# Two scatter views, later weight loads, and a middle layer among the last gates, in an attention and mixture-of-experts kernel

## The chip, the cores and the metric

The kernel runs on one core of one Trainium2 chip. A core has a matrix engine (TensorE, PE in the profile; PEld is its weight load), a vector engine (VectorE, DVE), a scalar engine (ScalarE, ACT), a general engine (GpSimd, POOL) and a queue engine (SyncE, SP), which here mainly starts DMA transfers. A letter q behind an engine's name (POOLq, SPq) stands for its sequencer. The metric is the device time of one execution in microseconds (us). A profiled execution gives the trace from which the tables below come.

## The reference

The reference is an attention block followed by a mixture of experts. The attention has 8 batches of 8 heads, 576 positions of 64 numbers; half of the heads see the last 32 positions, the other half every 32nd. Its output x (4608 rows of 512 numbers) goes to the experts. Every row takes one of 8 experts, and each expert is two layers with a ReLU between them:

```python
logits = np.einsum('bsd,de->bse', x, w_gate)
local_gate = 1.0 / (1.0 + np.exp(-np.einsum('bsd,de->bse', x, w_local).squeeze(-1)))
for b in range(B):
    prev_e = -1
    for s in range(S):
        fresh_e = int(np.argmax(logits[b, s]))
        if s == 0 or local_gate[b, s] < 0.5:
            e = fresh_e
        else:
            e = prev_e if prev_e >= 0 else fresh_e
        prev_e = e
        ...                                     # p = softmax(logits[b, s])
        h = np.maximum(x[b, s] @ w1[e], 0.0)    # 512 -> 1024
        out[b, s] = p[e] * (h @ w2[e])          # 1024 -> 512
```

So a row keeps the expert of the row before it unless its local gate is under one half. All is in 32-bit floats.

## The kernel before

The kernel computes the attention, two heads at a time ("pairs" of heads, 32 in all), stores x to a buffer xd in HBM, and works out the choice of each row: `gates` multiplies x by the gate weights, `choices` turns the result into codes and probabilities, and `route` sorts the rows by expert into tiles of 128. An expert tile then gathers its rows from xd by an indirect DMA (`gather`), turns them with the PE's transpose (`turn_x`), runs the first layer (`hidden`), the second (`output`), scales by the probability and scatters the rows to the output with an indirect DMA (`scatter`). Six tiles of the first three batches come first (units 0 to 5); they fill the time in which the last choices are routed. Then come pairs of tiles that share an expert (computed with seven products instead of eight), two mixed tiles between them, up to four single tiles, and at last the "late" pairs, as many as there are, each in an `If`.

The output is one tensor, and every scatter writes somewhere in it:

```python
    def scatter(self, y, rd, i):
        self.nc.gpsimd.indirect_dma_start(out=self.out, in_=y, in_offset=None, bounds_check=N - 1, oob_is_err=False,
                                          out_offset=bass.IndirectOffsetOnAxis(ap=rd.si[:, i:i + 1], axis=0))
```

The framework orders two writes of one tensor, so a scatter waits until the one before it has landed.

The end of the attention, where `n` counts pairs of heads and runs three steps past the last; `psX` is a pool of two PSUM banks that transposes, gates and choices use in turn:

```python
        done = pairs[n - 3][0].b if n >= 3 and pairs[n - 3][0].pair == PAIRS - 1 else None
        if done is not None:
            gates(done)
        yield n, st["pe"].ins
        if 0 <= n - 1 < len(pairs):
            values(pairs[n - 1][0])
        if done is not None:
            choices(done)
        if 0 <= n - 1 < len(pairs):
            u = pairs[n - 1][1]
            values(u)
            if u.i2 == 1:
                store_x(u.b, u.grp)
        if 0 <= n - 2 < len(pairs):
            u = pairs[n - 2][0]
            turn_x(u.b, u.pair)
```

`turn_x(0)` of the first expert tile is called one step before the last gates (`n == PAIRS * (B - BE) - 1` in the caller). After the attention all eight PSUM banks become one ring, `pse`; the first two are those of psX:

```python
    def later(self, ctx):
        self.banks = Banks(ctx.enter_context(self.tc.tile_pool(name="pse", bufs=1, space=PSUM)))
        self.banks.ring.used = 2
        # ... a third set of weights (w1x, w2x) and buffers of the pairs

    def hidden(self, j):
        nc, u = self.nc, self.U[j]
        w1, xT, hT = self.sets[u["set"]][0], u["xT"], u["hT"]
        for g in range(FK // self.HB):                      # two halves
            ps = self.bank()
            for i in range(self.HB):                        # four blocks of 128 in each
                c = slice((g * self.HB + i) * P, (g * self.HB + i + 1) * P)
                for kk in range(DK):
                    ins = nc.tensor.matmul(ps[:, i * P:(i + 1) * P], lhsT=w1[:, kk, c],
                                           rhs=xT[:, kk * P:(kk + 1) * P], start=(kk == 0), stop=(kk == DK - 1))
            nc.scalar.activation(hT[:, g * self.HB:(g + 1) * self.HB], ps.rearrange("p (i m) -> p i m", i=self.HB),
                                 Act.Relu)
        return ins.ins

    def output(self, j):                                     # plain tiles; mixed ones left out here
            for kk in range(FK):
                ins = nc.tensor.matmul(ps, lhsT=hT[:, kk], rhs=w2[:, kk, :], start=(kk == 0), stop=(kk == FK - 1))
        nc.scalar.activation(y, ps, Act.Copy, scale=u["pt"][:, 0:1])
        self.scatter(y, u["rd"], u["cols"][0])
        return ins.ins
```

How a unit runs and when it starts the weights of later ones (`self.last` is the first late pair; `weights(j)` gives four loads of 1 MB, two of w1 and two of w2; an `If` is opened around each `run(j)` of a late pair):

```python
    def unit(self, j, loads, nxt, step=lambda ins: None):
        # ...
        # first layer; then the first half of loads; step; turn_x of nxt; second layer; the other half; step

    def run(self, j, step=lambda ins: None):
        for k in self.gathers.get(j, []):
            self.gather(k)
        if j == self.last:
            for piece in self.weights(j + 1):
                piece()
        loads = self.weights(j + 2) if j + 2 < (self.last if j < self.last else len(self.U)) else []
        # ...
        self.unit(j, loads, self.turns.get(j, []), step)

    def early(self, second, check):
        def step(ins):
            with self.tc.issue_after(ins):
                next(second, None)
        for j in range(NE - 1):
            self.run(j, step)
        assert next(second, None) is None
        check()
```

`check` is the bounds check on the sums of the attention. Four VectorE operations (`ok` twice, `low`, `one`), one matmul and one more VectorE operation make one number, `bad`; if it isn't zero, the whole work is done again in a careful way. With these inputs it is zero.

```python
    nc.vector.tensor_scalar(ok, flat, SUM_LO, None, Alu.is_ge)
    nc.vector.scalar_tensor_tensor(ok, flat, SUM_HI, ok, Alu.is_le, Alu.mult)
    nc.vector.tensor_reduce(low, ok, axis=AX.X, op=Alu.min)
    nc.vector.memset(one, 1.0)
    nc.tensor.matmul(ps[0:1, 0:1], lhsT=low, rhs=one, start=True, stop=True)
    nc.vector.tensor_scalar(bad, ps[0:1, 0:1], -1.0, float(P), Alu.mult, Alu.add)
```

`issue_after(ins)` tells the scheduler to place what stands in the block behind the instruction named. The scheduler decides the order within each engine's queue otherwise.

Of the kernel before, what the change touches and what calls it, by code (L numbers as in the profile page):

```python
# [18 lines left out]
P = 128  # L19
# [99 lines left out]
@with_exitstack  # L119
def attention_then_scomoe(ctx: ExitStack, tc: tile.TileContext, q, k, vl, vs, wg, w1, w2, out):  # L120


    nc = tc.nc
    once = ctx.enter_context(tc.tile_pool(name="once", bufs=1))
    dram = ctx.enter_context(tc.tile_pool(name="dram", bufs=1, space=DRAM))
    xd = dram.tile([N, DX], F32, name="xd")
    c = Consts(tc, once)
    sums = once.tile([P, B * PAIRS * 2, 2, 3], F32, name="sums")
    nc.gpsimd.memset(sums, 1.0)
    bad = once.tile([1, 1], I32, name="bad")  # L130

    passes(tc, False, q, k, vl, vs, wg, w1, w2, out, xd, c, sums, bad)
    again = nc.values_load(bad[0:1, 0:1], min_val=0, max_val=P,
                           skip_runtime_bounds_check_because="a count of partitions")
    with tc.If(again > 0):
        passes(tc, True, q, k, vl, vs, wg, w1, w2, out, xd, c, sums, bad)
# [56 lines left out]
def passes(tc, careful, q, k, vl, vs, wg, w1, w2, out, xd, c, sums, bad):  # L193
    with ExitStack() as ctx:
# [7 lines left out]
        ex = Experts(ctx, tc, xd, w1, w2, out, c, r1, r2)  # L202
        with ExitStack() as part:
            psX = part.enter_context(tc.tile_pool(name="psX", bufs=2, space=PSUM))
            rp = part.enter_context(tc.tile_pool(name="rp", bufs=1))
            first = route(tc, rp, psX, BE, c, codes, r1, early)
            pieces = ex.weights(0) + ex.weights(1)
            for n, ins in attention(part, tc, careful, psX, q, k, vl, vs, wg, xd, c, codes, sums):
                n -= PAIRS * BE + 3

                if n == 0 or n >= 3:
                    with tc.issue_after(ins):
                        next(first, None)
                if n == PAIRS * (B - BE) - 1:
                    ex.banks = psX
                    ex.turn_x(0)
                if n in PIECES:
                    pieces.pop(0)()
                if 10 <= n < 10 + AHEAD:
                    ex.gather(n - 10)  # L220
        with ExitStack() as part:
            ex.later(ctx)
            rp = part.enter_context(tc.tile_pool(name="rp2", bufs=1))
            ex.early(route(tc, rp, ex.banks, B, c, codes, r2, early),
                     lambda: None if careful else bounds(tc, rp, ex.banks, sums, bad))
# [20 lines left out]
def attention(ctx, tc, careful, psX, q, k, vl, vs, wg, xd, cc, codes, sums):  # L246
# [8 lines left out]
    psS = ctx.enter_context(tc.tile_pool(name="psS", bufs=2, space=PSUM))  # L255
# [130 lines left out]
    def values(u):  # L386
# [5 lines left out]
        for h, order in ((0, reversed(range(m))), (1, range(m))):  # L392
            for i in order:
                o = (h * m + i) * V1 + (pad if h else 0)
                c = 0 if h else VW - w
                nc.tensor.matmul(ps[0:w, o:o + w], lhsT=u.e[0:kb, h, i * w:(i + 1) * w],  # L396
                                 rhs=vt[0:kb, u.i2, u.t0 + i, c:c + w], start=True, stop=True)
# [23 lines left out]
    def turn_x(b, pair):  # L421
# [7 lines left out]
        for ts in ((0, 1, 2), (3, 4, 5)) if grp == 0 else ((0, 1, 2), (3, 4)):  # L429
            w = LQ if grp == 0 else SBLK[ts[0]][1] * SP  # L430
            ps = psX.tile([P, 512], F32, name="xps")
            for i, t in enumerate(ts):
                nc.tensor.transpose(ps[:, i * w:(i + 1) * w], src[0:w, t, i2 * P:(i2 + 1) * P], ident[0:w, 0:w])  # L433
# [7 lines left out]
    def gates(b):  # L441
# [3 lines left out]
        for a in range(2):  # L445
            s = slice(a * (S // 2), (a + 1) * (S // 2))
            pg = psX.tile([P, 512], F32, name="xps")
            for kk in range(DK):
                nc.tensor.matmul(pg[kk * GC:(kk + 1) * GC, 0:S // 2], lhsT=wgs[:, kk, :], rhs=xT[:, kk, s],  # L449
                                 start=True, stop=True)  # L450
            nc.scalar.copy(out=gl[:, s], in_=pg[:, 0:S // 2])
        st["gl", b] = gl

    def choices(b):
        gl = st["gl", b]
        ps = psX.tile([P, 512], F32, name="xps")
        for t in range(LT):
            nc.tensor.matmul(ps[0:LQ, t * (E + 1):(t + 1) * (E + 1)], lhsT=gl[:, t * LQ:(t + 1) * LQ],  # L458
                             rhs=sel, start=True, stop=True)
# [36 lines left out]
    for n in range(len(pairs) + 3):  # L496
# [8 lines left out]
        done = pairs[n - 3][0].b if n >= 3 and pairs[n - 3][0].pair == PAIRS - 1 else None  # L505
        if done is not None:
            gates(done)
        yield n, st["pe"].ins
        if 0 <= n - 1 < len(pairs):
            values(pairs[n - 1][0])  # L510
        if done is not None:
            choices(done)
# [5 lines left out]
        if 0 <= n - 2 < len(pairs):  # L518
            u = pairs[n - 2][0]
            turn_x(u.b, u.pair)  # L520
# [223 lines left out]
class Experts:  # L744
# [14 lines left out]
    def __init__(self, ctx, tc, xd, w1, w2, out, c, r1, r2):  # L759
        self.tc, self.nc = tc, tc.nc  # L760
        self.xd, self.w1, self.w2, self.out, self.c = xd, w1, w2, out, c
# [36 lines left out]
        for j, u in enumerate(self.U):  # L798
# [3 lines left out]
            self.turns.setdefault(ahead - 1, []).append(j)  # L802
# [4 lines left out]
    def later(self, ctx):  # L807

        self.banks = Banks(ctx.enter_context(self.tc.tile_pool(name="pse", bufs=1, space=PSUM)))
        self.banks.ring.used = 2  # L810
# [194 lines left out]
    def hidden(self, j):  # L1005
        nc, u = self.nc, self.U[j]
        w1, xT, hT = self.sets[u["set"]][0], u["xT"], u["hT"]
        for g in range(FK // self.HB):
            ps = self.bank()
            for i in range(self.HB):  # L1010
                c = slice((g * self.HB + i) * P, (g * self.HB + i + 1) * P)
                for kk in range(DK):
                    ins = nc.tensor.matmul(ps[:, i * P:(i + 1) * P], lhsT=w1[:, kk, c],  # L1013
                                           rhs=xT[:, kk * P:(kk + 1) * P], start=(kk == 0), stop=(kk == DK - 1))
            nc.scalar.activation(hT[:, g * self.HB:(g + 1) * self.HB], ps.rearrange("p (i m) -> p i m", i=self.HB),
                                 Act.Relu)
        return ins.ins
# [18 lines left out]
    def scatter(self, y, rd, i):  # L1036
        self.nc.gpsimd.indirect_dma_start(out=self.out, in_=y, in_offset=None, bounds_check=N - 1, oob_is_err=False,  # L1037
                                          out_offset=bass.IndirectOffsetOnAxis(ap=rd.si[:, i:i + 1], axis=0))

    def unit(self, j, loads, nxt, step=lambda ins: None):  # L1040
# [7 lines left out]
        else:  # L1048
            self.end = (self.hidden_mixed if "halves" in u else self.hidden)(j)
# [13 lines left out]
    def run(self, j, step=lambda ins: None):  # L1063
# [3 lines left out]
        if j == self.last:  # L1067
            for piece in self.weights(j + 1):
                piece()
        loads = self.weights(j + 2) if j + 2 < (self.last if j < self.last else len(self.U)) else []  # L1070
# [4 lines left out]
    def early(self, second, check):  # L1075
# [9 lines left out]
        check()  # L1085
# [77 lines left out]
```

## Time and profile before

| | |
|---|---|
| device time, median of three | 706.21 us (704.58 to 706.42) |
| profiled span, first to last instruction | 704.3 us |
| mean granted TensorE clock | 0.983 |
| attention | up to about 163.7 us of the span |
| six early tiles | 163.7 to 258.6 |
| pairs and two mixed tiles | 258.6 to 571.7 |
| four single tiles | 571.7 to 629.1 |
| two late pairs | 629.1 to 680.2 |
| HBM traffic | 164.00 MB read, 19.55 MB written |

The page of the profile gives busy shares of each engine, the chain of work that ended last, and groups of instructions by line. The table of stretches cuts the span where one wants and gives busy times and the DMA share for each cut; the timeline lists instructions in order of time, with the idle time before each in brackets and what ended it. An fp32 matmul is recorded as two passes, so the 32 matmuls of one first layer appear as x64. Times in the timeline are from the start of the span.

### The profile page before, as it was taken

How to read it: one execution, taken by the hardware profiler on the slowest of the kernel's cores; microseconds unless marked ns; L12 is line 12 of the kernel's file. 1: busy time of each engine (PE TensorE's matmuls, PEld its weight loads, DVE VectorE, ACT ScalarE, POOL GpSimd, SP SyncE). 2: the span in 40 equal slices, each digit the busy share in tenths (PEclk: the TensorE clock that was granted, in tenths of full speed). 3: DMA queues.
4: the chain of work that ended last, by engine and by line, in shares of the span. 5: the costliest groups of instructions: out<-in, count | busy, mean ns of one | idle time of the engine just before them, and what ended most of it. 6: DMA issues, size and time to landing. Idle time of an engine off the chain costs nothing.

```text
span 704.3 us, 13289 instructions
## 1 busy us (share of the span) xinstructions
PE 674.3 (96%) x5258; PEld 579.0 (82%) x5258; DVE 401.4 (57%) x901; ACT 193.3 (27%) x360; POOL 102.5 (15%) x101
## 2 busy tenths in 40 slices
PE   8999999999999999999999999999999999999960
PEld 8999899987677779999499995899999986779950
DVE  6777888774374157576456955277578530307640
ACT  3454534442111123312132221313313311113310
POOL 1000002000003511120223202021122011020210
PEclk9999999999999999999999999999999999999995
DMA  9988788994878996885768767675688759468350
GB/s 344 374 305 289 228 282 294 370 329 146 306 265 291 322 398 260 275 310 218 269 246 306 250 238 278 212 229 191 210 298 293 269 181 338 162 229 309 124 207 7
DMA packets 75227, 184.01 MB, mean 261 GB/s; under 512 B 9743, under 2 KB 19471, under 8 KB 75153
## 3 DMA queue, kind: packets, MB, share of 16 engines
q1 hardware_dynamic: 68464, 162.10, 65.5%
q0 software_dynamic: 6400, 20.63, 8.4%
q8 instruction: 45, 0.74, 0.4%
q10 hardware_dynamic: 288, 0.31, 0.2%
q14 instruction: 30, 0.24, 0.1%
HBM read 164.00 MB, written 19.55 MB: 261 GB/s over the span
## 4 chain that ended last, share of the span: by engine, by line
PE 65%; issue 16%; DMA 11%; DVE 4%; ACT 1%; POOL 0%; SPq 0%; POOLq 0%; DVEq 0%
PE bank L896 32%; PE vps L396 9%; DMA out_dram<-y,si 7%; PE bank L1013 6%; PE bank L1031 6%; PE sps L349 5%; PE bank L1027 2%; PE xps L433 2%; DMA w2t<-in_w_dram 2%; DMA w1t<-in_w_dram 1%; PE xps L449 1%; PE xps L458 1%; DMA vlt<-in_vl_dram 1%; DMA xd<-ex 0%; DVE e L356 0%
## 5 line engine op out<-in xcount | busy, mean ns | idle before, releaser
L1037 POOL DMA_INDIRECT out_dram<-y,si x38 | 49.9, 1312 | 291.7 <-DVE y L964 135.5
L839 POOL DMA_INDIRECT xg<-xd,gi x42 | 49.4, 1175 | 288.8 <-DMA xd<-ex 114.1
L1013 PEld LDWEIGHTS bank<-xgT,w1t 128*128 128x128 f32 x640 | 72.6, 192 | 2.4 <-issue 1.9
L1013 PE MATMUL bank<-xgT,w1t 128*128 128x128 f32 x640 | 73.6, 276 | 0.3 <-DVE lt L461 0.3
L1031 PE MATMUL bank<-w2t,hT 128*128 128x512 f32 x160 | 70.3, 592 | 0.0
L1031 PEld LDWEIGHTS bank<-w2t,hT 128*128 128x128 f32 x160 | 29.6, 190 | 33.5 <-issue 33.5
L931 DVE TENSOR_TENSOR part<-bank,part 128x512 f32<-128x512 f32 x13 | 9.0, 692 | 80.6 <-ACT part L928 80.6
L896 PE MATMUL bank<-xs,t 128*128 128x128 f32 x416 | 50.7, 275 | 0.0
L896 PE MATMUL bank<-t,hs 128*128 128x256 f32 x208 | 49.2, 379 | 0.2 <-DVE hs L870 0.2
L896 PEld LDWEIGHTS bank<-xs,t 128*128 128x128 f32 x416 | 48.5, 192 | 0.0
L896 PEld LDWEIGHTS bank<-xT,w1t 128*128 128x128 f32 x384 | 45.7, 192 | 2.6 <-issue 2.1
L896 PE MATMUL bank<-xT,w1t 128*128 128x128 f32 x384 | 47.4, 276 | 0.0
L896 PE MATMUL bank<-xs,w1t 128*128 128x128 f32 x384 | 46.8, 275 | 0.0
L921 DVE TENSOR_TENSOR h<-bank,part 128x512 f32<-128x512 f32 x39 | 27.0, 692 | 34.7 <-ACT part L933 22.9
L349 PE MATMUL sps<-qt,kt 64*128 64x96 f32 (+2 forms) x704 | 45.7, 275 | 0.7 <-issue 0.6
L896 PE MATMUL bank<-w2t,h 128*128 128x256 f32 x192 | 45.4, 379 | 0.0
L896 PE MATMUL bank<-w2t,hs 128*128 128x256 f32 x192 | 45.4, 379 | 0.0
L896 PEld LDWEIGHTS bank<-xs,w1t 128*128 128x128 f32 x384 | 44.8, 192 | 0.0
L349 PEld LDWEIGHTS sps<-qt,kt 64*128 64x128 f32 (+2 forms) x704 | 40.1, 183 | 5.3 <-issue 3.2
L896 PEld LDWEIGHTS bank<-t,hs 128*128 128x128 f32 x208 | 39.4, 190 | 5.9 <-issue 0.6
L961 ACT ACTIVATE part<-bank,pt 128x256 f32<-128x256 f32 x39 | 18.5, 475 | 92.4 <-PE bank L896 92.4
L353 ACT ACTIVATE e<-sps 128x576 f32<-128x576 f32 (+1 forms) x64 | 40.0, 651 | 12.6 <-PE sps L349 12.2
(280 smaller groups left out, 1108.9 us busy)
## 6 DMA issues: line engine op xcount, KB each, us to landing
w1t<-in_w_dram SPq DMA_DIRECT2D x52, 1024.0 KB
w2t<-in_w_dram SPq DMA_DIRECT2D x52, 1024.0 KB
kt<-in_k_dram SPq DMA_DIRECT2D x15, 608.0 KB
qt<-in_q_dram SPq DMA_DIRECT2D x15, 576.0 KB
vlt<-in_vl_dram SPq DMA_DIRECT2D x8, 780.0 KB
w1x<-in_w_dram SPq DMA_DIRECT2D x6, 1024.0 KB
w2x<-in_w_dram SPq DMA_DIRECT2D x6, 1024.0 KB
vst<-in_vs_dram SPq DMA_DIRECT2D x8, 650.0 KB
```

Of the source, the lines that this page charges most:

```text
L349: st["pe"] = nc.tensor.matmul(ps[0:kb, h, i * w:(i + 1) * w], lhsT=kt[r, u.i2, c:c + kb], rhs=qt[r, u.i2, c:c + w], start=True, stop=True)
L353: nc.scalar.activation(ev, ps[0:kb, :, 0:m * w], Act.Exp, bias=0.0, scale=1.0 / DH ** 0.5)
L396: nc.tensor.matmul(ps[0:w, o:o + w], lhsT=u.e[0:kb, h, i * w:(i + 1) * w], rhs=vt[0:kb, u.i2, u.t0 + i, c:c + w], start=True, stop=True)
L433: nc.tensor.transpose(ps[:, i * w:(i + 1) * w], src[0:w, t, i2 * P:(i2 + 1) * P], ident[0:w, 0:w])
L839: self.nc.gpsimd.indirect_dma_start(out=u["xg"][:, a] if "pair" in u else u["xg"], out_offset=None, in_=self.xd[0:u["rows"]], in_offset=ba ...
L896: self.end = fn(*args, **kw).ins
L921: nc.vector.tensor_tensor(to, ps, add, op=Alu.add)
L961: nc.scalar.activation(to, ps, Act.Copy, scale=g[r])
L1013: ins = nc.tensor.matmul(ps[:, i * P:(i + 1) * P], lhsT=w1[:, kk, c], rhs=xT[:, kk * P:(kk + 1) * P], start=(kk == 0), stop=(kk == DK - 1))
L1027: ins = nc.tensor.matmul(ps[s], lhsT=hT[:, kk, s], rhs=w[:, kk, :], start=(kk == 0), stop=(kk == FK - 1))
L1031: ins = nc.tensor.matmul(ps, lhsT=hT[:, kk], rhs=w2[:, kk, :], start=(kk == 0), stop=(kk == FK - 1))
L1037: self.nc.gpsimd.indirect_dma_start(out=self.out, in_=y, in_offset=None, bounds_check=N - 1, oob_is_err=False, out_offset=bass.IndirectOff ...
```

## The change

The change has four parts.

- The output is split into two views that the framework takes as disjoint, and the scatters write them in turn. A scatter then waits for the last but one and not for the last. (The rows of two scatters are never the same, as every row has one tile.) The careful second pass begins with a read of both views, so that it waits for the scatters of the first.
- A late pair starts the four loads of the next late pair only, at its own beginning. Before, the first late pair started those of the second and, half by half, of the third, and so on.
- The first layer of the first expert tile is cut into four pieces of two blocks and put among the last transposes, gates and choices of the attention, pinned one behind the other, with its results in the PSUM banks of the attention's scores. `turn_x(0)` comes two steps earlier, and `turn_x(1)` right after the last choices. The ring of eight banks starts at the seventh.
- The bounds check is put in an `issue_after` block behind the last instruction of the early tiles.

```diff
+    views = dram_disjoint_views(out, 2)
+    passes(tc, False, q, k, vl, vs, wg, w1, w2, views, xd, c, sums, bad)
     ...
     with tc.If(again > 0):
+        seen = once.tile([1, 2], F32, name="seen")
+        for i, v in enumerate(views):
+            nc.gpsimd.dma_start(out=seen[:, i:i + 1], in_=v[0:1, 0:1])
+        nc.gpsimd.tensor_copy(seen, seen)
     ...
     def scatter(self, y, rd, i):
-        self.nc.gpsimd.indirect_dma_start(out=self.out, in_=y, ...
+        self.views.append(self.views.pop(0))
+        self.nc.gpsimd.indirect_dma_start(out=self.views[0], in_=y, ...
```

```diff
     def run(self, j, step=lambda ins: None):
-        if j == self.last:
+        if self.last <= j < len(self.U) - 1:
             for piece in self.weights(j + 1):
                 piece()
-        loads = self.weights(j + 2) if j + 2 < (self.last if j < self.last else len(self.U)) else []
+        loads = self.weights(j + 2) if j + 2 < self.last else []
```

```diff
+            psS = part.enter_context(tc.tile_pool(name="psS", bufs=2, space=PSUM))
+            fill = ex.begin(psS)
     ...
-                if n == PAIRS * (B - BE) - 1:
+                if n == PAIRS * (B - BE) - 3:
                     ex.banks = psX
                     ex.turn_x(0)
     ...
+            ex.turn_x(1)
     ...
+    def filling():
+        with tc.issue_after(st["end"].ins):
+            st["end"] = next(fill)
+
+    def after():
+        return tc.issue_after(st["end"].ins)
     ...
+        last = done == B - 1
         if done is not None:
-            gates(done)
+            with after() if last else nullcontext():
+                gates(done)
         yield n, st["pe"].ins
         if 0 <= n - 1 < len(pairs):
             values(pairs[n - 1][0])
+        if last:
+            filling()
         if done is not None:
-            choices(done)
+            with after() if last else nullcontext():
+                choices(done)
+        if last:
+            filling()
     ...
         if 0 <= n - 2 < len(pairs):
             u = pairs[n - 2][0]
-            turn_x(u.b, u.pair)
+            if n - 1 == len(pairs):
+                filling()
+                with after():
+                    turn_x(u.b, u.pair)
+                filling()
+            else:
+                turn_x(u.b, u.pair)
     ...
-        self.banks.ring.used = 2
+        self.banks.ring.used = 6
     ...
+    def begin(self, pool):
+        for i, self.begun in enumerate(self.hidden_blocks(0, pool)):
+            if i % 2:
+                yield self.begun
     ...
         # in early():
-        check()
+        with self.tc.issue_after(self.end):
+            check()
```

`hidden_blocks` is `hidden` as a generator: it yields after each block of four matmuls and can take its PSUM from a pool that is passed in. `st["end"]` is set by the matmuls of values, transposes, gates and choices.

## The prediction

> **What bounds the kernel now.** I read the page's busy shares first, then the table of stretches, then the timeline at the two places where TensorE (PE) is not busy, then the chain of waits.
>
> ```profile
> PE 674.3 (96%) x5258; PEld 579.0 (82%) x5258; DVE 401.4 (57%) x901; ACT 193.3 (27%) x360; POOL 102.5 (15%) x101
> ```
>
> PE is the bound: 674.3 of 704.3 us. So a change that leaves PE's work as it is, as this one does, can win at most the 30.0 us in which PE is idle. The table of stretches says where they are (columns: stretch, length, then busy time of PE, PEld, DVE, ACT, POOL, granted clock, DMA share, GB/s).
>
> ```profile
> 17.60:152.00 134.40, 133.28 (x1619) 120.76 (x1619) 101.56 (x357) 64.88 (x132) 4.09 (x4) 0.99 0.89 307
> 152.00:164.00 12.00, 10.56 (x103) 8.49 (x101) 6.39 (x24) 4.97 (x10) 0.08 (x1) 1.00 0.73 245
> 164.00:258.60 94.60, 94.60 (x604) 69.91 (x603) 44.12 (x119) 11.82 (x20) 21.84 (x17) 1.00 0.82 291
> ...
> 572.00:629.00 57.00, 57.00 (x331) 41.76 (x330) 7.59 (x13) 7.26 (x12) 5.96 (x6) 1.00 0.65 230
> ```
>
> PE never stops between 164.0 and 680.2 but for some 0.9 us in all at the mixed tiles. The change touches two of the idle places: the hand-over from attention to experts (152 to 164) and the end (680.2 to 704.3, 24.1 us without one matmul). First the hand-over, in the timeline (start, us, engine, line; in brackets the idle time before and who ended it):
>
> ```profile
> 158.83 0.87 PE L433 MATMUL xps<-ident,xs 108*128 108x108 f32 x5 [0.58 <-ACT xT L439]
> 160.12 1.59 PE L449 MATMUL xps<-xT,wgs 128*32 128x288 f32 x16 [0.42 <-ACT xT L439]
> 163.69 7.41 PE L1013 MATMUL bank<-xgT,w1t 128*128 128x128 f32 x64 [0.30 <-DVE lt L461]
> 167.78 0.36 DVE L235 TENSOR_SCALAR ok<-sums 128x384 f32<-128x384 f32 x1 [3.51 <-DMA xd<-xs]
> 169.13 0.51 DVE L238 TENSOR_REDUCE low<-ok 128x1 f32<-128x384 f32 x1
> 169.56 0.20 DVE L479 TENSOR_TENSOR codes<-code,fr 96x48 f32<-96x48 f32 x1
> ```
>
> See that the bounds check (ok, low) already lies inside the chain of the last choices here: VectorE stood 3.51 us until the stores of xs had landed. It did no harm, because PE had 7.41 us of the first middle layer to do meanwhile and wanted codes only at 171.03. Then the end:
>
> ```profile
> 675.01 5.55 SPq L830 DMA_DIRECT2D w2t<-in_w_dram  x2
> ...
> 680.24 0.47 ACT L961 ACTIVATE y<-bank,pt 128x256 f32<-128x256 f32 x1 [2.97 <-PE bank L896]
> 682.64 1.01 POOL L1037 DMA_INDIRECT out_dram<-y,si  x1 [3.55 <-DMA out_dram<-y,si]
> ```
>
> The last y is there at 680.71, but its scatter starts at 682.64: it waited for the scatter before it. The list of DMA issues for the last 24 us gives its landing, and the list of the If's control instructions what GpSimd does then:
>
> ```profile
> out_dram<-y,si POOLq DMA_INDIRECT x1, 6.6
> ```
>
> ```profile
> L226 POOLq EVENT_SEMAPHORE  x4: 17/43/6563, 682.6 to 689.4; - x4
> L226 POOLq INC_SWDGE_SEM  x1: 1780/1780/1780, 689.4 to 689.4; - x1
> ```
>
> 6.6 us to land, at 689.24; GpSimd stands in a wait of 6.56 us for it and goes on at 689.4. From there 15.06 us of control work lead to 704.3. Beside the scatter the DMA engines still load w2t: the second of the two issues at 675.01 came at 680.2, and 683 to 685 shows 418 GB/s. It is for the third of the late pairs, which does not exist with these inputs: only two late pairs run (PE reads w1x, then w1t, and then ends).
>
> [...] the scatter at 652.61 lands after 2.77 us in the chain of waits. [...] what stands behind a waiting instruction waits too. The 3.51 us above show it.
>
> **The change part by part.** PE's work is the same instructions, so each part is worth only the idle time it removes.
>
> *Two views.* The last scatter no longer waits for the one before. The one before started 0.28 us after its y (y ended 677.31 + 0.48 = 677.79, start 678.07). So the last starts at 680.71 + 0.28 = 680.99 and not at 682.64: 1.65 us on the path. Elsewhere the waits between scatters sum to 13.6 us (17.2 in all less this 3.6), but GpSimd stood there off the path, since PE had no idle time: 0.
>
> *Weights one pair ahead.* In the first late pair nothing moves: the built order has the same eight loads after one another, only the If test of the second pair now stands between them. The four loads for a third pair (w1t from 658.29, w2t from 675.01) leave the second pair's block and stand behind a test that fails: 4 MB are not loaded. With the DMA engines empty the last scatter should land in 2.77 instead of 6.6 us: 3.8 us on the path.
>
> *A side effect.* The build also puts six of the eight output matmuls of the third single tile behind the whole block of the fourth. Same work, same PE time; the fourth tile's xgT is needed at 608.18 + 2 x 0.86 = 609.9 and is there (its transposes end at 608.2, the copy takes 0.69). I count 0[...].
>
> *First middle layer among the gates.* What it fills: from 155.50 to 163.69 are 8.19 us, and the work in it, from the chain of waits, is 2.25 (values) + 0.44 (transposes of xg, at their undisturbed length) + 0.50 + 0.50 (transposes of xs) + 1.11 (gates, undisturbed as at 29.27) + 0.95 (choices) = 5.75. So 2.44 us can be filled, and the 64 passes of the middle layer (7.14 us, 111.6 ns each) are more than enough. What it costs: with these passes spent early, PE comes to the output layer at 155.50 + 5.75 + 7.14 + 0.44 (transposes of the second tile) = 168.85, and that stands on PSUM bank 0, where the second tile's transposes have just been written. It has to wait until VectorE has copied them away. In the built VectorE order this copy stands behind ok, gmx, fr, ok, ex, eq, low, eq, gsm, code, gsm, one, code, gsm: the pin on the bounds check has not moved it behind the choices; it now stands right after lt, ahead of gmx. The first ok again waits for the stores of xs. Those come some 0.4 us later than before (the copy of the first xgT and two small operations now go ahead of the last xs on VectorE), so ok starts at about 168.1. From ok to the copy, in steps of start to start as the timeline before has them (0.28 and 0.47 for the two ok, 0.43 for low, 0.05 to 0.13 for the rest): 2.3 us, so the copy runs from 170.4 to 171.1. PE stands from 168.85 to 171.15, 2.3 us. Then one output matmul (0.86), codes (1.14), seven output matmuls (6.01) and 0.2 for switching: 179.36, against 179.69 before. Gain 0.3 us of the possible 2.4.
>
> *Sum.* 1.65 + 3.8 + 0.3 = 5.8 us, or 0.8%.
>
> **Rivals.** First, the stall at output is smaller: if the stores of xs land before lt, only lt and 2.3 us of VectorE's queue are left, PE waits 1.2 us, and the part gains 1.4: 699.3. The DMA share of 0.5 in 164 to 167, with nothing under way but these stores and one gather, speaks against it. Second, the stall is longer or other waits come (ReLU before the copies of gl on ScalarE, PSUM banks in turn): the part loses 1 us, 701.7. ScalarE has room (4.97 of 12 us), which speaks against much. Third, the end doesn't shrink, because another engine or transfer ends last: PE's branch over the second pass takes 6.5 us, from 682.6 to 689.1, ScalarE and SyncE come at 688.8 and 688.6. If these do not move, GpSimd, which before went on to its last step at 696.7, may come 5.5 us earlier and is still the last at 691.2; so I hold this for unlikely. If it were so, 704 or 705. Fourth, the late pairs' weights come too late now: but their loads wait for the same PE releases as before, and w1t and w2t of the second late pair are released 5.2 us earlier by the side effect.
>
> **Range and chances.** 706.2 - 5.8 = 700.4 us. The end is the surer part (4.5 to 6), the hand-over the less sure (-1.5 to +2.4): 698.4 to 703.0. For 2% the time would have to fall below 692.1, and no idle time that the change touches yields 14 us; above 720.3 nothing leads.
>
> **What would show it.** Two views: the last scatter within 0.4 us of its y. Weights: no load issued after about 635, the last scatter lands in under 3.3 us. The end: some 15 us from landing to the last instruction, as before. Hand-over: PE without idle from 156 to 168.5, then 1 to 3 us of idle ahead of the first output matmul, ended by VectorE's copy of xgT, with ok ahead of it waiting on xs. Wrong would be: PE idle between the singles and the late pairs, a wait of 5 us or more in the landing, or no stall at the output layer.

## The result and the profile after

The changed kernel takes 705.13 us (median of 5, 703.23 to 706.23) against 705.36 us: a ratio of 0.9992, 95% interval 0.997 to 1.0014. So the time stayed where it was; 700.4 us had been predicted, 698.4 to 703.0 as the range.

The page shows that the work is the same. The stretches show where time was lost (columns: stretch, length, then busy time of PE, PEld, DVE, ACT, POOL, granted clock, DMA share, GB/s).

```profile
PE 674.8 (96%) x5258; PEld 580.4 (83%) x5258; DVE 401.5 (57%) x901; ACT 193.1 (27%) x360; POOL 99.2 (14%) x101
...
HBM read 159.80 MB, written 19.55 MB: 255 GB/s over the span
```

```profile
17.60:154.05 136.45, 135.34 (x1624) 122.71 (x1625) 101.96 (x357) 65.32 (x133) 4.09 (x4) 0.97 0.89 305
154.05:164.00 9.95, 9.81 (x100) 9.54 (x98) 5.85 (x20) 4.22 (x8) 0.95 (x1) 1.00 0.84 277
164.00:260.20 96.20, 94.48 (x608) 68.65 (x607) 44.17 (x122) 12.49 (x23) 20.46 (x16) 1.00 0.81 288
```

The 4.2 MB of useless loads are gone, PE has work between 154 and 164 us, and it has lost 1.72 us in the stretch behind, where it had none idle before. The mean clock of the attention is 0.97 and not 0.99. The timeline at the hand-over of the changed kernel (start, us, engine, line; the idle time before in brackets):

```profile
169.86 0.36 DVE L245 TENSOR_SCALAR ok<-sums 128x384 f32<-128x384 f32 x1 [0.77 <-DMA xd<-xs]
172.14 0.65 DVE L889 COPY xgT<-xps 128x512 f32<-128x512 f32 x1
```

```profile
172.89 1.10 PE L1076 MATMUL bank<-w2t,hT 128*128 128x512 f32 x2 [1.72 <-issue]
```

This is the predicted stall: ok waits for the stores of xs, the copy of xgT stands behind it in VectorE's queue, and PE behind the copy. Then the end: the last y and its scatter, the scatter's landing (the list of DMA issues), and GpSimd's control instructions at the If.

```profile
681.81 0.47 ACT L993 ACTIVATE y<-bank,pt 128x256 f32<-128x256 f32 x1 [2.97 <-PE bank L928]
682.56 1.01 POOL L1084 DMA_INDIRECT out_dram<-y,si  x1 [1.91 <-ACTq L236]
```

```profile
out_dram<-y,si POOLq DMA_INDIRECT x1, 4.9
```

```profile
L236 POOLq EVENT_SEMAPHORE  x4: 17/43/4930, 682.5 to 687.6; - x4
L236 POOLq INC_SWDGE_SEM  x1: 1780/1780/1780, 687.7 to 687.7; - x1
```

The last scatter starts 0.28 us after its y, as predicted, but lands in 4.9 us and not in 2.77. From there 14.9 us lead to the end, 15.06 before. From the end of the last matmul to the last instruction it is now 20.7 us, against 24.1. So 3.5 us were won at the end, and the whole time did not fall.

I use two measures below. The *hand-over* is the time from the last transposes of xl to the first product with cum behind the first output; it is 154.70 to 179.62 = 24.92 us in the kernel before, 156.75 to 181.25 = 24.50 after. The *end* is the time from the last matmul's end to the last instruction.

### The profile page after: what moved, and what is told of

It reads as the page before. It is cut to its first block, busy times and chain, and to the rows that moved or that the text cites. A ratio compares the mean times of both kernels' runs of the same rounds, so it can differ in the third digit from the quotient of the medians.

```text
span 702.4 us, 13279 instructions
## 1 busy us (share of the span) xinstructions
PE 674.8 (96%) x5258; PEld 580.4 (83%) x5258; DVE 401.5 (57%) x901; ACT 193.1 (27%) x360; POOL 99.2 (14%) x101
## 4 chain that ended last, share of the span: by engine, by line
PE 86%; DMA 5%; DVE 4%; issue 1%; ACT 1%; SPq 1%; POOL 0%; DVEq 0%; POOLq 0%
PE bank L928 46%; PE bank L1076 10%; PE bank L1051 9%; PE vps L406 9%; PE sps L359 5%; PE bank L1072 2%; PE xps L443 2%; DMA w2t<-in_w_dram 2%; DMA w1t<-in_w_dram 1%; PE xps L460 1%; PE xps L476 1%; DMA vlt<-in_vl_dram 1%; DMA xd<-xs 1%; DVE e L366 1%; DVE xs L417 0%
## 5 line engine op out<-in xcount | busy, mean ns | idle before, releaser
L871 POOL DMA_INDIRECT xg<-xd,gi x42 | 46.2, 1099 | 301.4 <-DVE rc L416 151.2
L1051 PEld LDWEIGHTS bank<-xgT,w1t 128*128 128x128 f32 x576 | 65.4, 192 | 2.0 <-issue 1.7
L1051 PE MATMUL bank<-xgT,w1t 128*128 128x128 f32 x576 | 66.2, 276 | 0.0
```

Of the source, the lines that this page charges most:

```text
L871: self.nc.gpsimd.indirect_dma_start(out=u["xg"][:, a] if "pair" in u else u["xg"], out_offset=None, in_=self.xd[0:u["rows"]], in_offset=ba ...
```

## The experiments

Each time is a median of all runs beside runs of the kernel before on the same chip. Those were 705.12 us for the first four kernels, 704.62 for the next four, 706.08 for the last eight; so kernels of different groups are compared by their ratios, not by their times.

### The whole and its three parts

At first I knew from the one trace of the changed kernel that TensorE's clock had been at one half for 6.8 us near 100 us and for 3.4 us in the kernel before. So I held two explanations (T1 and T2 where the texts name them so): this difference is chance, and hides the gain; or the changed kernel brings it on, say by the small new tile `seen`, which moves later buffers by 32 B. Four kernels: the change again, and each part alone on top of the kernel before.

```diff
 views_only    the two views and `seen`, nothing else of the change
 weights_only  if self.last <= j < len(self.U) - 1: ... weights(j + 1); loads only if j + 2 < self.last
 gates_only    begin/filling/after, turn_x earlier, ring at 6, bounds check in issue_after(self.end)
```

> The changed kernel once more. Theory T1 (the saving is there and is hidden by the half-clock spell of TensorE near 100 us[...]): over more runs the clock of the runs spreads as it does for the kernel before, and the ratio settles near 0.995 (3 to 4 us faster), with runs of low mean clock the slow ones. Rival T2 (the 32 bytes by which the new tile moves every later tile make the loads and the attention slower): the ratio stays at 0.999, the first vlt load again lands in about 6.4 us (6.0 before), and the attention ends 2 us later in this profile too, whatever the clock.

> The kernel before with the two views alone. The prediction's step: the last scatter starts 0.28 us after its y and not 1.9 us, 1.65 us less, and the landing shares the engines with the useless w2t load, so 6.6 us from issue as before, or ends where it ended before if the load decides: between 0 and 1.7 us faster (ratio 0.998 to 1.000). T2 expects the 2 us loss in the attention here, since this kernel has the new tile, so 1 to 2 us slower (1.002).

> The kernel before with the weights one pair ahead alone. The last scatter still waits for the one before it, which now lands in 2.8 instead of 3.7 us; its own landing is 2.8 us if only the load slowed it (prediction: 4.7 us faster in all, ratio 0.993), or 4.9 us as in the changed kernel's profile if something else in the end keeps it (2.6 us faster, 0.996). T2 expects no loss in the attention, as no tile moves.

> The kernel before with the first middle layer among the gates and the pinned check, one output tensor and the loads of before. The hand-over gains 0.3 to 0.5 us up to the end of the first output layer, with a stall of 1.7 to 2.3 us ahead of it: ratio 0.999 to 1.000, the same within the noise.

| kernel | us | ratio to before, 95% | hand-over | end |
|---|---|---|---|---|
| after_again | 705.29 | 0.9999 (0.9984 to 1.0014) | 28.48 | 19.8 |
| views_only | 705.44 | 1.0005 (0.9996 to 1.0014) | 24.92 | 23.5 |
| weights_only | 702.34 | 0.9966 (0.9954 to 0.9978) | 24.93 | 21.0 |
| gates_only | 708.76 | 1.0059 (1.0042 to 1.0075) | 27.18 | 24.1 |

The weights win 0.34%, the views alone nothing, and the gates part *costs* 0.59%. In after_again and views_only, which have the tile `seen`, the last transposes of xl start at 154.91 and 153.74 us, and at 154.70 in the kernel before, so the second explanation has no loss to explain. Neither was the main one: the loss sits in the part that was to fill idle time. Its hand-over is 2.3 us longer in this profile, though TensorE starts the last transposes of xl no later. In the traces of the kernel before and of the changed one, all changes in the record of the granted clock lie whole multiples of 3.413 us apart (1 and 170 of them before, 2 and 170 after). Stretches of gates_only, cut at such a change and every 3.41 us from it:

```profile
164.52:167.93 3.41, 3.41 (x35) 3.41 (x35) 0.21 (x1) 0.00 (x0) 0.00 (x0) 1.00 0.17 51
167.93:171.35 3.42, 0.63 (x4) 0.34 (x3) 3.34 (x19) 0.72 (x2) 0.00 (x0) 1.00 0.71 267
171.35:174.76 3.41, 3.41 (x14) 1.89 (x12) 0.51 (x2) 0.00 (x0) 0.94 (x1) 0.50 0.73 188
174.76:178.17 3.41, 3.41 (x9) 1.63 (x9) 3.16 (x5) 0.00 (x0) 0.00 (x0) 1.00 0.62 247
```

```profile
171.00 1.72 PE L1071 MATMUL bank<-w2t,hT 128*128 128x512 f32 x2 [2.79 <-issue]
```

PE is busy for 0.63 of 3.42 us while it waits for VectorE (the stall is 2.79 us here); in the next stretch it is busy throughout, but at a clock of 0.50. In after_again the same lasts two stretches:

```profile
169.17:172.59 3.42, 0.99 (x4) 0.30 (x2) 2.95 (x18) 0.72 (x2) 0.00 (x0) 1.00 0.86 281
172.59:176.00 3.41, 3.41 (x14) 2.39 (x14) 1.29 (x3) 0.00 (x0) 0.94 (x1) 0.50 0.86 208
176.00:179.42 3.42, 3.42 (x5) 1.35 (x4) 3.28 (x5) 0.00 (x0) 0.00 (x0) 0.50 0.53 212
```

And in the profile of the changed kernel that stood at the head, the same stall of 1.72 us happened to lie across a border, 0.50 us idle on one side and 1.23 on the other, and the clock stayed:

```profile
168.25:171.66 3.41, 2.91 (x27) 2.68 (x26) 2.01 (x10) 0.64 (x2) 0.00 (x0) 1.00 0.15 23
171.66:175.08 3.42, 2.19 (x15) 1.34 (x15) 1.95 (x13) 0.08 (x1) 0.94 (x1) 1.00 1.01 312
175.08:178.49 3.41, 3.41 (x9) 1.60 (x9) 3.27 (x6) 0.00 (x0) 0.00 (x0) 1.00 0.92 367
```

So theory A: a stall of this size makes the clock fall for one or two stretches of 3.41 us, each of which costs up to half its length, 1.7 us, an estimate from the recorded 0.50. That the stall is the cause was a guess from these traces; they don't show what sets the clock. In those of the kernel before and the changed one only 1.00 and 0.50 are recorded. The spells of 0.50 before the last matmul are one stretch long (3.41 us: kernel before, gates_only) or two (6.83: changed kernel, after_again). The shortest stall within one stretch that a half clock followed is the 1.59 us of pause (below). Rival B: the order of the gates costs time in another way, and the half clock comes by chance, as I then took it to near 100 us.

### Filling the wait, and lengthening it

gates_filled and busy_wait put products that nothing reads into PE's wait of gates_only. VectorE's order was to stay, and with it the wait.

```diff
 # gates_filled: into a bank of the new ring, 20 products; busy_wait: into a bank of the scores, 12 products
+    ps, xT = psS.tile([P, 2, 512], F32, name="sps"), ex.U[0]["xT"]
+    with tc.issue_after(ex.end):
+        for _ in range(12):
+            ex.begun = nc.tensor.matmul(ps[:, 1, 0:P], lhsT=xT[:, 0:P], rhs=xT[:, 0:P], start=True, stop=True)
```

> The gates part alone, as in gates_only, with twenty products of 128x128 that nothing reads put into TensorE's program between the turn of the second tile and the codes, where gates_only stood idle for 2.8 us. They change no wait of the rest by more than some tenths of a us. Theory A (the idle time at the hand-over lets the granted clock fall to one half for one or two windows of 3.41 us, and each costs up to 1.7 us): with TensorE busy there the clock stays at 1.0 through 170 to 180 us and the time falls from 708.8 us to that of the kernel before or just under it, 704.5 to 706. Rival B (the order of the gates costs the time itself, and the low clock near 175 us is chance): the twenty products change nothing or add up to 0.5 us, 708.5 to 709.5, with a low clock there as often as in gates_only.

> The gates part alone, as in gates_only, with twelve products of 128x128 that nothing reads[...] into a bank of PSUM that is free already, ahead of the wait for VectorE; in gates_filled they stood behind that wait and made it longer. VectorE's order and so the wait itself stay. Theory A[...]: the idle share of the windows at 165 to 175 us stays under 0.3, no half clock there, hand-over of 24.5 to 25 us, and the time falls from 708.8 to 704.6 to 705.6 us. Rival B (the order costs the time by itself): 708.3 to 709.3.

gates_filled missed its aim: 711.46 us, 1.0079 (1.0066 to 1.0092). The timeline shows why; the products themselves waited:

```profile
172.24 7.57 PE L1128 MATMUL bank<-xgT 128*128 128x128 f32 x40 [2.96 <-DVE codes L492]
```

They write into a bank of the new ring, and PE could begin them only when VectorE was done with codes. So here the products lengthened the stall (2.96 us idle, then 7.57 us for 40 passes, where busy_wait's 24 took 2.84 at a clock of 1.00) instead of filling it. It tells nothing between A and B. busy_wait, with a bank of the old pool, does (the products, then the stretches):

```profile
171.33 2.84 PE L230 MATMUL sps<-xgT 128*128 128x128 f32 x24
```

```profile
167.66:171.07 3.41, 3.41 (x36) 3.41 (x35) 0.98 (x5) 0.00 (x0) 0.00 (x0) 1.00 0.08 24
171.07:174.49 3.42, 3.31 (x31) 3.15 (x30) 2.63 (x16) 0.72 (x2) 0.21 (x1) 1.00 0.73 249
174.49:177.90 3.41, 3.41 (x18) 2.02 (x17) 2.73 (x5) 0.00 (x0) 0.73 (x1) 1.00 1.02 318
```

PE is busy through the wait, the clock stays at 1.00, and the time is 706.82 us, a ratio of 1.0006 (0.9996 to 1.0017) where gates_only has 1.0059. Products that compute nothing win 0.53%, 3.7 us. The hand-over is 25.38 us, 0.46 longer than in the kernel before: the products took 2.84 us and covered a bit more than the wait. By ratio this is what A expects (its 704.6 to 705.6 us were written beside a kernel before at 705.1); B is out: the order of the gates without the stall costs 0.17% at most by the interval, where the whole gates part costs 0.59%.

pause is the test from the other side: the kernel before, without any part of the change, and with a wait in the same place.

```diff
     # in step, at its first call only
+    nc.gpsimd.tensor_copy(self.late[0:LQ, 0:E], codes[:, 0, 0])
+    for _ in range(8):
+        nc.gpsimd.memset(self.late[:, 0:384], 0.0)
+    with self.tc.issue_after(ins):
+        ins = nc.tensor.matmul(self.banks.ring[6][0:1, 0:1], lhsT=self.late[:, 0:1], rhs=self.late[:, 0:1],
+                               start=True, stop=True).ins
     with self.tc.issue_after(ins):
         next(second, None)
```

> The kernel before, with no part of the change, and with a pause: ahead of the product that turns the codes at the hand-over, TensorE does one product of one element that waits for a chain of eight memsets on GpSimd begun when the codes are ready; it should stand idle for 2.0 to 2.7 us near 171 to 173 us. Theory A: a half clock of one or two windows after it, where the kernel before never had one, and 2.2 us for the pause plus 1.3 to 3.4 for the clock: 708.4 to 710.6. Rival B (the clock doesn't answer to the pause): 706.8 to 707.6.

```profile
168.84:172.25 3.41, 3.41 (x33) 3.41 (x32) 1.74 (x12) 0.60 (x1) 1.92 (x6) 1.00 0.09 5
172.25:175.66 3.41, 1.82 (x20) 1.48 (x19) 0.66 (x2) 0.60 (x1) 1.61 (x4) 1.00 0.71 225
175.66:179.08 3.42, 3.42 (x8) 1.68 (x6) 3.09 (x7) 0.00 (x0) 0.10 (x1) 0.50 0.97 394
```

711.13 us, 1.0066 (1.0041 to 1.0091). PE was idle for 1.59 us in one stretch, 0.47 of it, less than was meant, and a clock of 0.50 followed for 3.41 us; the hand-over is 28.39 us, 3.47 more than in the kernel before. Idle time of 1.6 us cost 3.5 there. The whole time grew by 4.7 us by ratio, within A's 3.5 to 5.6 (its 2.2 plus 1.3 to 3.4) and outside B's 2.2; where the last 1.2 us lie was not settled.

Eleven profiles have a stall at the hand-over, and they fall into two groups. With an idle share of the worst stretch of 3.41 us of 0.26 (late_all and one_view_late, below), 0.36 (the changed kernel's first profile) and 0.44 (no_second_one, 2.74 us of stall across a border) there is no half clock; with 0.47 (pause), 0.56, 0.62, 0.63, 0.71, 0.72 and 0.82 one or two stretches of it come right behind. (Where no change of clock lies near, the borders are counted back from the one at the end in steps of 3413 ns, the recorded length of the half clock in the kernel before.)

Three of them separate what the idle time costs from what the clock costs, as they have the order of the changed kernel and nearly the same stall. With 2.74 us of stall and the clock up (no_second_one) the hand-over is 25.53 us; with 2.79 us and one stretch at half clock (gates_only) it is 27.18; with 2.64 us and two stretches (no_second_two) 28.61. So the stall alone leaves the hand-over 0.6 us longer than in the kernel before, and the clock adds 1.7 and 3.1 us.

### Taking the wait away

```diff
 # late_check
-    nc.vector.tensor_scalar(ok, flat, SUM_LO, None, Alu.is_ge)
+    with tc.issue_after(turned):        # turned: VectorE's reduce to pt of the second tile
+        nc.vector.tensor_scalar(ok, flat, SUM_LO, None, Alu.is_ge)
 # late_all: this, and
-    nc.vector.memset(one, 1.0)
+    with tc.issue_after(turned):
+        nc.vector.memset(one, 1.0)
```

> The changed kernel with the first instruction of the bounds check pinned behind VectorE's reduce for the second tile's gates, so that the copy of the second tile (xgT) comes before the bounds check, and TensorE doesn't wait for it at the first output product. Theory A: no idle time at the hand-over, so no half clock at 170 to 180 us; against the kernel before the gates part then gains some 2 us instead of losing 3.6, and with weights (-3.0 measured alone) the time is 699.5 to 701. Rival B: only the idle time goes (1.7 to 2.4 us of 705.3), and whatever else the gates part costs stays: 702.9 to 703.6.

> The changed kernel with the whole bounds check, its memset of one too, pinned behind VectorE's reduce for the second tile's gates. In late_check the memset had taken the place of ok at the head of VectorE's queue and waited there for the write of xs (1.84 us) with all of the gates' work behind it. With it behind, codes are ready some 1.8 us earlier and TensorE is idle for 0.3 to 1.0 us instead of 2.1. Theory A: idle share of the worst window under 0.3, no half clock at 170 to 180 us, hand-over of 23.0 to 23.7 us against 24.9 in the kernel before, so 702.7 (views_weights) less 1.2 to 1.9: 700.8 to 701.5. Rival B (gates part costs some 3 us whatever the wait): 702.5 to 703.5, as late_check.

late_check missed its aim: 703.63 us, 0.9981 (0.9969 to 0.9993), with a stall of 2.12 us and a half clock behind it. The time is near B's, but as the stall was still there, it doesn't decide. VectorE's timeline of late_check:

```profile
167.15 0.21 DVE L481 COPY lt<-xps 96x54 f32<-96x54 f32 x1 [7.77 <-PE xps L478]
169.20 0.06 DVE L252 MEMSET one<- 128x1 f32 x1 [1.84 <-DMA xd<-xs]
169.20 0.20 DVE L484 TENSOR_REDUCE gmx<-lt 96x6 f32<-96x48 f32 x1
```

The wait for the stores of xs belongs to none of the check's data; as its small tiles lie in a pool that is opened when the attention's are closed, I take it for a wait for memory. In gates_only ok waited 1.84 us for these stores; with ok moved away, the memset of a 128x1 tile waited the same 1.84 us and held the choices in its turn. In late_all nothing of the check is left there:

```profile
169.65 0.21 DVE L482 COPY lt<-xps 96x54 f32<-96x54 f32 x1 [7.77 <-PE xps L479]
169.89 0.20 DVE L485 TENSOR_REDUCE gmx<-lt 96x6 f32<-96x48 f32 x1
```

```profile
172.81 1.18 PE L573 MATMUL bank<-ident,codes 96*64 96x96 f32 x12 [0.88 <-DVE pe L896]
```

The choices follow lt at once, PE stalls for 0.88 us, 0.26 of its stretch of 3.41 us, the clock stays at 1.00, and the hand-over is 23.47 us, 1.45 shorter than before. 701.04 us, 0.992 (0.9904 to 0.9936): the best version that computes everything, and faster than both kernels. Beside views_weights and two_views_b (below), which lack only the gates part, this is 2.0 to 2.8 us by the ratios, where the hand-over shows 1.45; the intervals are wide enough to cover the difference.

### The end

views_weights (and later two_views_b, the same kernel) has the two views and the weights without the gates part; one_view_b is weights_only again; one_view_late is late_all with one view. no_second, and no_second_two again, is the changed kernel with the careful second pass and the branch to it left out, so without the fallback; no_second_one is the same with one view.

> The kernel before with the two views and with the weights begun one pair ahead, without the gates part. Parts that add up as predicted: the last scatter starts 0.3 us after its y and not 1.9, lands in 3.8 as in weights_only: 702.3 - 1.6 = 700.7. Rival (the landing is set by something that starts at a fixed time after y, so that an earlier scatter only lands more slowly, as 7.4 against 6.6 us in views_only): 701.9 to 702.5, no gain over weights_only.

> The changed kernel without the second, careful pass and the branch that decides on it (its answer is left unread): it leaves out the fallback for sums out of bounds. If the instruction fetches of the jump over that pass are what keeps the last scatter's landing at 3.8 to 4.9 us, it lands in 2.8 us, as scatters do in mid-run, and the time falls by 1.0 to 2.1 us for that, plus what the reading of the answer takes. Rival (the landing is that of any scatter at the end of the work): 3.8 to 4.9 us again.

> late_all with the scatters into one view, as in the kernel before. If the two views are worth nothing once the weights are begun one pair ahead (702.73 with, 702.34 without), it takes the same as late_all within 0.7 us. If they are worth the 1.65 us of the prediction, it is slower by that, 702.4 to 703.1.

> The changed kernel without the second, careful pass (as no_second, with two views), beside no_second_one. Left out: the fallback for sums out of bounds and the reading of its answer. Theory V1 (an earlier scatter is paid back because DMA engines that fetch instructions for the jump over the second pass finish their share late): without the jump the views bring nearly all of the predicted 1.65 us, so this takes 697.5 to 698.5 and no_second_one 1.2 to 2.0 us more. Rival V2 (the wait for the previous scatter overlaps something else and the views are worth at most 0.5 us anywhere): within 0.6 us of no_second_one.

> As no_second_two with all scatters into one view, so that the last waits for the landing of the one before it. Theory V1: slower than no_second_two by 1.2 to 2.0 us. Rival V2: by 0 to 0.6 us.

> The kernel before with two views and with the weights begun one pair ahead, with the second pass, beside one_view_b. Theory V1: its last scatter starts some 1.6 us sooner after y but lands in 4.5 to 5 us instead of 3.8, and the time is 0.3 to 1.0 us under that of one_view_b. Rival V2: within 0.5 us. The prediction's step: 1.65 us under.

> The kernel before with the weights begun one pair ahead, one view: 0.9966 of the kernel before in the first comparison, so 701.9 to 703.2.

| two views | one view | ratios to before | difference |
|---|---|---|---|
| views_weights 702.73 | weights_only 702.34 | 0.9960, 0.9966 | -0.4 us |
| two_views_b 702.20 | one_view_b 703.27 | 0.9948, 0.9959 | -0.8 us |
| late_all 701.04 | one_view_late 702.45 | 0.9920, 0.9948 | -2.0 us |
| no_second_two 699.07 | no_second_one 699.35 | 0.9891, 0.9901 | -0.7 us |

(The difference is that of the ratios, times 706. The intervals of all pairs overlap, all but the third's by more than half, and a mean of some 1 us is all that they give.) The profiles say the same with less scatter. The end is 23.7 to 24.1 us with one view and the useless loads (five kernels), 23.5 with two views and these loads, 21.0 to 21.8 with one view without them (three, mean 21.5), and 19.5 to 20.8 with both (six, mean 20.2). So the weights are worth 2.4 us of the end, and the views 1.3 on top, but only 0.4 while the loads are there: the scatter of views_only starts 0.28 us after its y and then takes 7.4 us to land, while the loads move another 1.05 MB beside its 0.28.

V1's forecast did not come: without the jump the views are worth no more, 0.7 us by the ratios and 0.8 by the ends (14.9 against 14.0 and 14.3). V2 is nearer in size. But the two kernels without the jump are not free of instruction fetches. What the DMA queues moved in the first 3.4 us of the last scatter, first of no_second_two, then of no_second_one:

```profile
q0 software_dynamic: 82, 0.27, 21.1%
q8 instruction: 1, 0.02, 1.6%
q14 instruction: 1, 0.01, 1.0%
```

```profile
q0 software_dynamic: 80, 0.26, 20.2%
```

In no_second_two, where the scatter starts 0.28 us after its y, two packets of instructions fall beside it, and its last packet is written 3.34 us after its start. In no_second_one it starts 1.98 us after its y, none falls beside it, and the last packet comes at 2.42 us. So of the 1.7 us won at the start 0.9 are paid back, as V1 has it, though the fetch here isn't the jump's; that it is the fetch which holds the scatter back is argued from the order of the packets.

The jump over the second pass has a cost of its own. In no_second the last scatter lands in 3.5 us, and from there it is 9.6 us to the end, where the other profiles have 14.9 to 15.2; the time is 698.06 us, 0.99 (0.9882 to 0.9919) against 0.9999 for the changed kernel. Its DMA queues from the last scatter on:

```profile
q0 software_dynamic: 85, 0.27, 2.3%
q8 instruction: 1, 0.02, 0.2%
q14 instruction: 2, 0.02, 0.2%
...
out_dram<-y,si POOLq DMA_INDIRECT x1, 3.5
```

and those of the changed kernel in the same place:

```profile
q0 software_dynamic: 82, 0.27, 2.8%
q14 instruction: 8, 0.07, 1.0%
q8 instruction: 3, 0.05, 0.9%
```

With the jump there are eleven packets of instructions instead of three. In the packet records of the changed kernel most of the scatter is written by 685.0, and the rest goes one packet after the other until 687.0, behind instruction packets of 16 KB that took up to 1.7 us each. That these hold back a few of the DMA engines is argued from this order; how far they set the landing was not measured by itself. It fits that no_second, at 3.5 us, still has two packets of instructions (8 and 16 KB) beside its scatter, and that no_second_one, which has none, would land after an estimated 2.9 us: its last packet at 2.42 us, plus the 0.4 to 0.6 us that lie between last packet and landing in the ten profiles where both are known.

## Why the prediction was wrong, step by step

*First middle layer among the gates: this step failed.* It was put at +0.3 us gained; alone it costs 0.59%, and its median is 3.6 us higher. What it said of the order was right: the stall ahead of the first output product, its length (2.3 us said; 1.72 to 2.79 in the six profiles with this order), that it ends with VectorE's copy and codes, and that ok ahead of them waits for xs. In the first profile, where the clock stayed up, the gain is 0.42 us, about the 0.3 said. The idle time to be filled was right too: late_all gains 1.45 us with 0.88 us of stall left, 2.33 together, against 2.44. The fault is in the line that sums it up: one output product at 0.86, codes at 1.14, seven products at 6.01, all at full clock. In after_again the same three took 1.22, 2.18 and 8.45 us:

```profile
171.75 1.22 PE L1076 MATMUL bank<-w2t,hT 128*128 128x512 f32 x2 [2.42 <-issue]
172.90 2.18 PE L570 MATMUL bank<-ident,codes 96*64 96x96 f32 x12
175.02 8.45 PE L1076 MATMUL bank<-w2t,hT 128*128 128x512 f32 x14
```

The change moves idle time from before 164 us, where it lay in pieces of 0.58 us at most (three of them stand in the prediction's own timeline), into one piece of 1.7 to 2.8 us, and the prediction counted the sum of idle time alone, with nothing for what the clock does after it. gates_only has a mean granted clock of 0.9803 in its timed runs, the kernel before 0.9847 in its own; times 707 us that is 3.1 of the 3.6 us. busy_wait and pause showed the cause from both sides.

None of the rivals had it. The second came nearest in sign, a loss of 1 us, and looked for it on ScalarE and in the PSUM banks.

*Two views: 1.65 us said.* The start 0.28 us after y is right in every profile with two views. They are worth nothing alone and about 1 us with the weights part. The step took for granted that a scatter that starts earlier lands earlier by as much.

*Weights one pair ahead: 3.8 us said, 0.34% or 2.4 us alone by the ratio and 2.4 by the end.* The loads went and the landing shortened as argued, but to 3.8 to 5.1 us in the five profiles where it was read, and not to the 2.77 of a scatter in mid-run. The term that was mis-sized is this landing. A scatter in mid-run does land in that time in the changed kernel too (2.8 us at 654 us), but the last one does not (4.9), and from it on eleven packets of instructions are moved.

*Side effect: 0 said, 0 found.* From the product with cum to the start of the last matmuls it is 498.65 us in the profile before and 498.59 after.

*15.06 us from landing to the end: right*, 14.9 to 15.2 in the nine profiles with a second pass whose landing was read. It is not fixed, though: 5.3 us of it go when the decision on the second pass is left out.

The sum: 5.8 us were said. Measured, the views and weights together are worth 0.40 and 0.52% (2.8 and 3.7 us) and the gates part costs 3.6 to 4.2 (by median, by ratio): nothing is left. The later end of the attention in the first trace (2.05 us) is, for about 1.6 us, the second stretch of half clock near 100 us. Profiles of kernels with the gates part have such stretches more often (7 of 11) than the others (2 of 7), but the last section shows that this goes with where the borders of the stretches happen to lie. And busy_wait, which has the gates part, takes 0.06% more than the kernel before.

## What to carry to other kernels

Idle time of the bound engine isn't a sum to be packed: here the kernel before had many gaps of 0.6 us at most with the clock at 1.00 (152 to 164 us), while one of 1.6 to 2.8 us was followed by a clock of 0.50 for one or two stretches of 3.41 us, which cost 1.7 us (one) and 3.1 (two) at the hand-over, unless a border between stretches parted the gap (twice). Before work is moved forward into gaps, ask what it leaves behind at the place where it stood, and give the remaining wait something to do. And pin a whole check aside, down to its smallest memset: whichever instruction of the check came first in VectorE's queue, ok in gates_only or the memset in late_check, stood there for 1.84 us, and the work of the choices behind it stood too.

## What the runs showed of the hardware that was not expected

In the stalls at the hand-over no half clock came after an idle share of up to 0.44 of a stretch of 3.41 us, and one came after each of 0.47 and more; with products in the wait whose results nobody reads (busy_wait) the clock stayed at 1.00, and 0.53% was won. A half clock of one or two stretches also comes near 100 us, in kernels with and without the gates part, with PE busy for 95% of the stretch before (3.25 of 3.41 us):

```profile
96.99:100.40 3.41, 3.25 (x31) 2.85 (x30) 3.38 (x12) 1.18 (x2) 0.00 (x0) 1.00 0.94 327
100.40:103.82 3.42, 3.42 (x19) 3.15 (x17) 1.94 (x11) 0.26 (x1) 0.00 (x0) 0.50 0.63 225
```

These are two stretches of the kernel before. The idle time of PE, 0.16 us, is far under the 0.47 of a stretch at the hand-over and does not explain the half clock; whether it comes goes with the place of the borders. The kernels all have one small product here:

```profile
97.36 0.38 PE L654 MATMUL xps<-over,ones 8*128 8x6 f32 x2
```

In ten of the 18 profiles the first border between stretches after the start of this product comes 1.86 to 3.41 us behind it (3.05 here), and in nine of them the half clock begins at that border; the tenth is weights_only, at 2.04. In the other eight it comes 0.20 to 1.77 us behind it, and none has a half clock there. Kernels with and without the gates part are on both sides. Why the clock falls there was not shown.
